# The fp32 doubling of the power tables on GpSimd in place of VectorE, with a higher threshold for early exponentials

## The chip, the cores and the metric

The kernel runs on one core of a Trainium2 chip. The core has TensorE (PE, matrix products), VectorE (DVE), ScalarE (ACT), GpSimd (POOL) and SyncE (SP, which issues DMAs here). The metric is the time of one execution on the device in microseconds (us).

## The reference, cut to what matters

Two mixers over the same x (2048 positions, 512 channels) are blended by a gate. A is attention with 32 heads of 16. B is a long convolution whose kernel is a sum of 128 complex powers per channel.

```python
x = A_x
g = _sigmoid((x * gate_w).sum(-1, keepdims=True))
a = _A_ref(x, A_wqkv, A_wo)      # scores -> softmax -> o @ wo, S = 2048, D = 512, H = 32
b = _B_ref(x, ...)               # dt = exp(log_dt); P = exp(dt*A*l); K = Re sum_n C*P*dB;
                                 # y = causal convolution of u with K, + u*Dskip
return g * a + (1 - g) * b
```

Inputs and output are bf16.

## The kernel before, in words

**Attention.** There are 32 blocks (4 quarters of 512 queries, 4 groups of 8 heads, 2 halves of a group), each of 16 key tiles by 4 row groups of PE: 2048 score tiles of 128 keys by 512 queries. Tiles go in groups of three, NG = 683 groups. For group g, `qk` writes three score banks (SC), `ex` (L913) is one exponential on ScalarE from SC to a ring of 15 tiles (ET), and `pv` multiplies ET by the values (VE) into one PSUM bank, OA. When a block ends, `norm_a` (L984) transposes OA on VectorE into OT, which frees OA for the next block; `norm_b` and `norm_c` normalise.

**Early sets.** For some key tiles VectorE computes the four exponentials itself, in a two-instruction approximation on bit patterns: `bits` (L949) turns a score bank into DZ, and `batch` (L960) makes two more shifted copies, DU and DZ, per set of four tiles. So a set is six VectorE instructions, and four groups have two tiles on ScalarE in place of three. `decide` starts a set only in the windows of groups in WIN (from group 180 on), only for the key tiles in VKT (four of sixteen per block up to group 640, then seven), and only if the idle time that the planner counts for VectorE has grown by a threshold. That threshold is `dvq()`: the first entry of DVQ whose flag is set (`scan1`, `scan0`, `S15`), else the last entry.

**The convolution.** `params` (all on VectorE) computes per channel the step L1 and the powers L2, L4, L8, then VL, marks `L8`, and goes on to L16, L32, L48 and their bf16 copies D16, D32, D48 (L1151). `base(qr)` builds for quarter qr (128 channels) a table of 16 consecutive powers in fp32 by doubling: two copies into FP (L1181), then products with L2, L4 and L8 into ft1 and ft2 and their sums and differences (all of them through the helper at L1007), and last a cast into the bf16 table B16 (L1204). `bases` runs the four quarters one after another. `table` multiplies B16 by D16, D32 and D48 in bf16 for pairs of blocks (eight pairs, two for each quarter): two copies (L1228) and 18 products and sums into PT, which goes to DRAM (`ptd`). A pair after the first waits for the kernel matrices (`K`, `kstage`, L1278) of the pair before it. `qload` reads PT back transposed (Qt), `sstage` makes the chunk states (from group 195 for blocks 0 to 7, from group 260 for 8 to 15; evicted at L1310), `scan` runs a recurrence over 30 chunks, twice, on VectorE (L1333 to L1340) with a DMA per chunk from GpSimd's queue (L1342), and `ystage` makes the outputs.

**What sets the order.** A planner writes out each engine's instruction stream in advance. Every step is a generator that yields the engine and an assumed duration; `Sched.fill` picks, engine by engine, what can start first, ties by priority. A product on 128 x n fp32 elements is booked with `dv(n)`:

```python
def dv(n, r=1):
    return .07 + n / 960 / r
```

whatever the engine, and each result with 0.085 us of latency. `AFTER` conditions order the planning alone; on the chip an instruction waits for semaphores of the data and the buffers that it uses. Each engine runs its stream in order.

Of the kernel before, what the change touches and what calls it, by code (L numbers as in the profile page):

```python
# [49 lines left out]
VSP = [len(k) * VSW for k in VKT]  # L50
VSAT = (168, 600)
WIN = ((180, 400, 2, 1), (400, 640, 2, 1), (640, 678, 3, 2))
DVQ = (("scan1", 0.2), ("scan0", 0.8), ("S15", 2.0), (None, 0.7))
BP = 2.2
DVCAP = 2.0
BUP = 1
# [33 lines left out]
class Prog:  # L90
# [107 lines left out]
    def op(self, eng, fn, R=(), W=(), c=.1, lat=.085, a=0, cfg=None):  # L198
        if self.cap is not None:
            self.cap.append((self.op, (eng, fn, R, W), dict(c=c, lat=lat, a=a, cfg=cfg)))  # L200
            return
        if cfg is not None:
            if cfg != self.cfg:
                c += TURN[cfg]
            self.cfg = cfg
        self.act += a
        self.log.append((self.op, self.q, (eng, fn, R, W)))
        deps = self._deps(eng, R, W)
        i = self.cnt[eng]
        at = self.tm[eng]  # L210
        for s, k in deps.items():
            at = max(at, self.fin[(s, k)] + (.03 if s == eng else .05))
        self.tm[eng] = at + c
        if eng == "DVE":
            self.busy += c
        self.fin[(eng, i)] = at + c + lat
        self.cnt[eng] += 1
        self._record(eng, fn, deps, eng, i, R, W)
        return at + c + lat
# [392 lines left out]
def dv(n, r=1):  # L612
    return .07 + n / 960 / r


def record(nc, p, B, ins):
# [135 lines left out]
    def dvq():  # L752
        return next(n for f, n in DVQ if f is None or f in sch.flag)

# [251 lines left out]
    def tt(eng, o, a, b_, f, R, W, c):  # L1006
        op(eng, lambda v: v.tensor_tensor(o(), a(), b_(), f), R, W, c=c)  # L1007
# [4 lines left out]
    def key(*ns):  # L1012
        return [(B[n], 0) for n in ns]
# [158 lines left out]
        sch.mark("scanpar")  # L1172

    def base(qr, eng):
        yield ("AFTER", "L8")
        FP, t1, t2, B16 = B["FP"], B["ft1"], B["ft2"], B[f"B16{qr}"]
        d0 = 128 * qr
        e8 = 128 * 8
        for l, n in ((0, "VV"), (1, "VL")):
            yield (eng, .38)  # L1180
            op(eng, lambda v, l=l, n=n: v.tensor_copy(FP(l, [[e8, 2], [8, 128]]), B[n](d0, [[D, 2], [1, 128]])), key(n), [(FP, 0)], c=.34)  # L1181
        for m, ln in ((2, "L2"), (4, "L4"), (8, "L8")):
            L = B[ln]
            for ch0 in range(0, 128, 64 if m == 8 else 128):
                nch = 64 if m == 8 else 128
                x = lambda ch0=ch0, m=m, nch=nch: FP(8 * ch0, [[e8, 2], [8, nch], [1, m]])
                ts = m * nch
                for ti, ri in ((t1, 0), (t2, 1)):
                    yield (eng, dv(2 * ts))
                    tt(eng, lambda ti=ti, ts=ts, nch=nch, m=m: ti(0, [[ts, 2], [m, nch], [1, m]]), x,  # L1190
                       lambda ri=ri, ch0=ch0, nch=nch, m=m, L=L: L(ri * D + d0 + ch0, [[0, 2], [1, nch], [0, m]]), ALU.mult,
                       [(FP, 0), (L, 0)], [(ti, 0)], dv(2 * ts))
                for part, f in ((0, ALU.subtract), (1, ALU.add)):
                    if m < 8:
                        o = lambda part=part, m=m: FP(part * e8 + m, [[8, 128], [1, m]])
                        W = [(FP, 0)]
                    else:
                        o = lambda part=part, ch0=ch0: B16(part * 2048 + ch0 * 16 + 8, [[16, 64], [1, 8]])
                        W = [(B16, (1, ch0))]
                    yield (eng, dv(ts))  # L1200
                    tt(eng, o, lambda part=part, ts=ts, nch=nch, m=m: t1(part * ts, [[m, nch], [1, m]]),
                       lambda part=part, ts=ts, nch=nch, m=m: t2((1 - part) * ts, [[m, nch], [1, m]]), f, [(t1, 0), (t2, 0)], W, dv(ts))
        yield (eng, 1.2)
        op(eng, lambda v: v.tensor_copy(B16(0, [[2048, 2], [16, 128], [1, 8]]), FP(0, [[e8, 2], [8, 128], [1, 8]])),  # L1204
           [(FP, 0)], [(B16, 0)], c=1.2)
        sch.mark(f"base{qr}")
# [439 lines left out]

    def bases():
        for qr in range(4):
            yield from base(qr, "DVE")

    for th, pr in ((norms(), 0), (qms(), 0), (projs(), 1), (gate(), .8), (ystage(), 2), (yloads(), 4), (params(), 2), (vscaled(0), 2.2), (vscaled(1), 2.2), (scan(), 3),
                   (bases(), BP), (table(), 2), (ublocks(), 4), (xyloads(), 4), (early(), 1.5), (reload(), 5), (outs(), 6)):
        sch.add(th, pr)
# [126 lines left out]
```

## Time and profile before

| what | value |
|---|---|
| median of the timed runs | 854.03 us (853.03 to 855.03, 2 runs) |
| the profiled execution, span from first to last instruction (no other time is listed for it) | 854.3 us |
| ScalarE busy | 826.1 us, 97%, 695 instructions |
| VectorE busy | 766.1 us, 90%, 1271 instructions |
| TensorE busy | 756.7 us, 89% |
| GpSimd busy | 44.0 us, 5%, 73 instructions |
| mean granted TensorE clock | 0.985 |

Busy time is the union of an engine's instructions. A row of a group of instructions gives the line, the engine, the operation, output<-inputs with shapes, the count, the busy time in us and the mean ns of one, and then the idle time just before them with what ended it. A row of the timeline gives the start and length in us. Lines of helpers (L1007, L632) carry many steps: tell them apart by the tiles.

### The profile page before, as it was taken

The page shows a single profiled execution, that of the slowest core. Times are in us where ns is not written, and L with a number is a line of the kernel's source. Part 1 is how long each engine was busy: PE and PEld are TensorE (multiplying, and loading weights), DVE is VectorE, ACT ScalarE, POOL GpSimd, SP SyncE. Part 2 cuts the span into 40 slices and gives each one's busy share as a digit, 9 for nine tenths or more (in the row PEclk, how much of TensorE's full clock was granted, in tenths as well). Part 3 has the DMA queues.
Part 4 walks back from the last instruction along what each step waited for, and adds up shares of the span by engine and source line. Part 5 has one row for each costly group of instructions (what it writes and reads, how often), then busy time and mean ns, then how long its engine had stood idle before and what let it go on. Part 6 is the DMA issues. An engine that isn't in the chain of part 4 may idle for free.

```text
span 854.3 us, 23568 instructions
## 1 busy us (share of the span) xinstructions
PE 756.7 (89%) x10301; PEld 296.5 (35%) x10301; DVE 766.1 (90%) x1271; ACT 826.1 (97%) x695; POOL 44.0 (5%) x73
## 2 busy tenths in 40 slices
PE   7888888788768999999999899889988899999986
PEld 3232332222212434343443344334442234443321
DVE  5799999999969988898898999999999978997994
ACT  6999999999979999999999999999999999999996
POOL 4000000000000000000010111101111100000000
PEclk9999999999989999899998999999999999999999
DMA  9400102942933498477394597248998425645120
GB/s 206 118 2 10 35 3 82 194 153 81 73 129 152 51 206 103 149 131 164 62 162 71 84 192 116 36 104 166 199 191 151 120 88 121 136 120 113 25 99 26
DMA packets 218168, 94.55 MB, mean 111 GB/s; under 512 B 185168, under 2 KB 205008, under 8 KB 216016
## 3 DMA queue, kind: packets, MB, share of 16 engines
q1 hardware_dynamic: 207408, 83.99, 45.6%
q0 software_dynamic: 8640, 7.87, 5.9%
q8 instruction: 81, 1.33, 0.6%
q10 hardware_dynamic: 2016, 1.18, 0.6%
q14 instruction: 23, 0.19, 0.1%
HBM read 35.17 MB, written 30.82 MB: 77 GB/s over the span
## 4 chain that ended last, share of the span: by engine, by line
ACT 66%; PE 23%; DMA 5%; DVE 4%; SPq 1%; issue 0%; ACTq 0%; DVEq 0%
ACT ET L913 65%; PE OA L632 9%; PE SC L632 7%; PE MB L632 7%; DMA gm_gd<-g 3%; DMA gm_ytd<-Yst 1%; DMA gm_ptd<-PT 1%; DVE DZ L949 1%; DMA Wq<-in_A_wqkv_dram 1%; DVE s L1333 1%; DVE s L1335 1%; DVE G L1340 0%; DVE s L1338 0%; DVE tt L1007 0%; SPq L1488 0%
## 5 line engine op out<-in xcount | busy, mean ns | idle before, releaser
L913 ACT ACTIVATE ET<-SC 128x1536 bf16<-128x1536 f32 (+1 forms) x683 | 817.8, 1508 | 15.1 <-PE SC L632 13.9
L632 PE MATMUL SC<-Qm,KT 32*128 32x512 bf16 x2048 | 276.5, 387 | 75.9 <-ACT ET L913 61.1
L632 PE MATMUL OA<-wm 128*32 128x256 bf16 (+3 forms) x2193 | 251.6, 341 | 1.2 <-DVE wm L685 1.2
L632 PE MATMUL OA<-ET,VE 128*32 128x512 bf16 x1800 | 181.6, 395 | 4.6 <-DVE OT L984 4.4
L949 DVE TENSOR_SCALAR DZ<-SC 128x512 uint16<-128x512 f32 x248 | 166.2, 685 | 19.1 <-PE SC L632 16.8
L632 PEld LDWEIGHTS SC<-Qm,KT 32*128 32x128 bf16 x2048 | 70.7, 91 | 291.8 <-ACT ET L913 233.9
L632 PEld LDWEIGHTS OA<-wm 128*32 128x32 bf16 (+2 forms) x2193 | 72.9, 95 | 33.8 <-issue 15.5
L632 PEld LDWEIGHTS OA<-ET,VE 128*32 128x32 bf16 x1800 | 46.1, 93 | 106.1 <-issue 98.4
L632 PE MATMUL MB<-X,Qt 64*128 64x32 bf16 x1024 | 74.5, 231 | 0.0
L632 PEld LDWEIGHTS MB<-X,Qt 64*128 64x128 bf16 x1024 | 57.7, 109 | 25.2 <-issue 23.0
L1310 DVE TENSOR_SCALAR SG<-MB 128x512 bf16<-128x512 f32 x64 | 43.9, 686 | 10.6 <-PE MB L632 9.8
L960 DVE TENSOR_SCALAR DZ<-DZ 128x2048 uint16<-128x2048 uint16 x62 | 42.5, 685 | 8.2 <-PE OA L632 8.2
L1342 POOL DMA_DIRECT2D SG<-G x60 | 33.0, 550 | 255.7 <-DVE G L1340 250.9
L1340 DVE TENSOR_TENSOR G<-s,s 128x512 f32<-128x512 f32 x60 | 41.2, 687 | 3.1
L960 DVE TENSOR_SCALAR DU<-DZ 128x2048 uint16<-128x2048 uint16 x62 | 42.3, 685 | 0.4
L1333 DVE TENSOR_TENSOR s<-G,MU 128x512 f32<-128x512 f32 x60 | 41.2, 687 | 1.0
L1338 DVE TENSOR_TENSOR s<-s,SG 128x512 f32<-128x512 f32 x60 | 41.1, 685 | 0.0
L1335 DVE TENSOR_TENSOR s<-G,MU 128x512 f32<-128x512 f32 x60 | 41.0, 683 | 0.0
L1007 DVE TENSOR_TENSOR ft<-FP,L 128x1024 f32<-128x1024 f32 (+1 forms) x32 | 34.4, 1084 | 0.1
L1007 DVE TENSOR_TENSOR PT<-tt,tt 128x1024 bf16<-128x1024 bf16 x48 | 32.8, 683 | 0.4
L632 PEld LDWEIGHTS MB<-Py,SG 128*32 128x32 bf16 x1024 | 29.6, 165 | 8.2 <-issue 4.1
L984 DVE STREAM_TRANSPOSE OT<-OA 128x512 f32<-128x512 f32 x32 | 22.8, 712 | 9.2 <-PE OA L632 8.8
(166 smaller groups left out, 625.6 us busy)
## 6 DMA issues: line engine op xcount, KB each, us to landing
gm_ptd<-PT SPq DMA_DIRECT2D x16, 1024.0 KB, 6.1
Py<-gm_ptd SPq DMA_DIRECT2D x32, 512.0 KB, 5.0
SG<-G POOLq DMA_DIRECT2D x60, 128.0 KB, 3.1
gm_kpd<-Kst SPq DMA_DIRECT2D x16, 256.0 KB, 3.5
Tt<-gm_kpd SPq DMA_DIRECT2D x128, 32.0 KB, 3.5
gm_xrd<-in_A_x_dram SPq DMA_DIRECT2D x1, 2048.0 KB, 13.2
X<-gm_xrd SPq DMA_DIRECT2D x8, 256.0 KB, 5.0
Wo<-in_A_wo_dram SPq DMA_DIRECT2D x4, 512.0 KB, 4.4
```

The lines of the kernel that those rows point to most:

```text
L632: op("PE", lambda t: t.matmul(out(), lhsT(), rhs(), start=start, stop=stop, skip_group_check=True, **kw), R, W, c=c, lat=.15, a=a, cfg=cfg)
L913: op("ACT", lambda a: a.activation(ET(512 * e, [[1, 512 * n]]), sc(0, [[1, 512 * n]]), AF.Exp, scale=DH ** -0.5), [(sc, i, g) for i in ran ...
L949: op("DVE", lambda v: v.tensor_scalar(z.u16(512 * k, [[1, 512 * n]]), sc(512 * na, [[1, 512 * n]]), XS, XB, ALU.mult, ALU.add), [(sc, na + ...
L960: op("DVE", lambda v: v.tensor_scalar(t.u16(0, [[1, 2048]]), z.u16(0, [[1, 2048]]), float(STEP[k][0]), None, ALU.add), R, W, c=.07 + 2048 ...
L984: op("DVE", lambda v: v.transpose(OT(512 * w, [[1, 512]]), OA(0, [[1, 512]])), [(OA, 0, b)], [(OT, w, b)], c=.64)
L1007: op(eng, lambda v: v.tensor_tensor(o(), a(), b_(), f), R, W, c=c)
L1310: op("DVE", lambda v, bank=bank, par=par, part=part: v.tensor_scalar(sg(2 * SGH + SGH * part + CB * k8 + 16 * par, [[2 * SGH, 32], [1, 16] ...
L1333: op("DVE", lambda v, g0=g0: v.tensor_tensor(s2(0, W), g0(0, W), MU(d0, [[0, 2], [1, 256]]), ALU.mult), [(g0, 0)] + key("MU"), [(s2, 0)], ...
L1335: op("DVE", lambda v, g0=g0: v.tensor_tensor(s3(0, W), g0(256, [[-256, 2], [1, 256]]), MU(D + d0, [[D, 2], [1, 256]]), ALU.mult), [(g0, 0) ...
L1338: op("DVE", lambda v, so=so: v.tensor_tensor(s2(0, W), s2(0, W), sg(so, W), ALU.add), [(s2, 0)] + ks, [(s2, 0)], c=F5)
L1340: op("DVE", lambda v, g1=g1: v.tensor_tensor(g1(0, [[1, 512]]), s2(0, [[1, 512]]), s3(0, [[1, 512]]), ALU.add), [(s2, 0), (s3, 0)], [(g1, ...
L1342: later("POOL", .3, 0, lambda so=so, g1=g1, c=c: dma("POOL", lambda e: e.dma_start(sg(so, [[1, 512]]), g1(0, [[1, 512]])), [(g1, 0)], [(sg ...
```

## The change

The doubling of all four quarters is issued to GpSimd. In the planning, quarters 2 and 3 may begin only when the tables of blocks 2 and 6 have been issued to their DMA. The last entry of DVQ, the threshold that holds until the flag `S15` or `scan0` is set, is 1.2 us in place of 0.7. The assumed durations are not changed.

```diff
-DVQ = (("scan1", 0.2), ("scan0", 0.8), ("S15", 2.0), (None, 0.7))
+DVQ = (("scan1", 0.2), ("scan0", 0.8), ("S15", 2.0), (None, 1.2))
...
     def base(qr, eng):
-        yield ("AFTER", "L8")
+        yield ("AFTER", f"pt{4 * qr - 6}" if qr >= 2 else "L8")
...
     def bases():
         for qr in range(4):
-            yield from base(qr, "DVE")
+            yield from base(qr, "POOL")
```

## The prediction

> **What bounds the kernel now.** I read the page's busy times first, then the exponentials by form, then all engines over six stages, then the same stages for L960 alone (two instructions for each early set on VectorE).
>
> ```profile
> PE 756.7 (89%) x10301; PEld 296.5 (35%) x10301; DVE 766.1 (90%) x1271; ACT 826.1 (97%) x695; POOL 44.0 (5%) x73
> ...
> L913 ACT ACTIVATE ET<-SC 128x1536 bf16<-128x1536 f32 x434 | 593.6, 1713 | 9.7 <-PE SC L632 9.3
> L913 ACT ACTIVATE ET<-SC 128x1024 bf16<-128x1024 f32 x249 | 242.0, 1151 | 5.4 <-PE SC L632 4.7
> ...
> 80.00:235.00 155.00, 126.29 (x1469) 41.26 (x1470) 151.14 (x245) 155.00 (x118) 0.00 (x0) 1.00 0.42 86
> 263.00:420.00 157.00, 150.83 (x1996) 64.28 (x1996) 140.74 (x236) 152.62 (x136) 1.05 (x2) 0.98 0.66 138
> ...
> 677.00:845.00 168.00, 153.72 (x2376) 58.98 (x2375) 141.56 (x233) 167.81 (x164) 0.53 (x1) 1.00 0.37 90
> ...
> 263.00:420.00 157.00, 23.68 (x35) 0.98 0.66 138
> 420.00:545.00 125.00, 8.88 (x13) 0.97 0.67 110
> 677.00:845.00 168.00, 40.45 (x60) 1.00 0.37 90
> ```
>
> The columns of the stage rows are PE, PEld, DVE, ACT and POOL with counts, then granted clock, DMA share and GB/s. ScalarE is busy 826.1 of the span's 854.3 us: the exponentials set the time. The span lies between the two timed runs (853.03 and 855.03), so I sum against 854.3 and add nothing around it.
>
> The time can fall in one way only, by more early sets: each takes four tiles off ScalarE. What one is worth: from 80 to 235 nearly all 118 activations have three tiles, 155.00 / 118 = 1.31 us each. From 677 to 845 there are 60 / 2 = 30 sets, so 120 activations of two tiles and 44 of three: (167.81 - 44 x 1.31) / 120 = 0.92 us. Four times 0.39 is 1.6 us a set. It can rise in one way too: VectorE being late with something that ScalarE needs.
>
> **The change, part by part.**
>
> *What VectorE loses.* All rows of the doubling, over four quarters, and some rows of its queue for the spacing:
>
> ```profile
> L1007 DVE TENSOR_TENSOR ft<-FP,L 128x1024 f32<-128x1024 f32 x24 | 29.0, 1217 | 0.1
> L1007 DVE TENSOR_TENSOR B<-ft,ft 128x512 bf16<-128x512 f32 x16 | 10.9, 683 | 0.1
> L1007 DVE TENSOR_TENSOR FP<-ft,ft 128x512 f32<-128x512 f32 x8 | 5.5, 686 | 0.1
> L1007 DVE TENSOR_TENSOR ft<-FP,L 128x512 f32<-128x512 f32 x8 | 5.5, 684 | 0.0
> L1204 DVE CAST B<-FP 128x2048 bf16<-128x2048 f32 x4 | 4.9, 1218 | 0.0
> L1007 DVE TENSOR_TENSOR FP<-ft,ft 128x256 f32<-128x256 f32 x8 | 3.3, 419 | 0.0
> L1181 DVE COPY FP<-VV 128x256 f32<-128x256 f32 x4 | 1.6, 397 | 0.0
> ...
> 79.92 0.39 DVE L1181 COPY FP<-VV 128x256 f32<-128x256 f32 x1
> ...
> 94.54 1.22 DVE L1007 TENSOR_TENSOR ft<-FP,L 128x1024 f32<-128x1024 f32 x1
> 95.67 0.68 DVE L1007 TENSOR_TENSOR L<-pt,pt 128x512 f32<-128x512 f32 x1
> 96.28 0.68 DVE L731 CAST VE<-MB 128x512 bf16<-128x512 f32 x1
> ...
> 99.62 0.42 DVE L1151 CAST D48.3_156<-L 128x512 bf16<-128x512 f32 x1
> ...
> 101.12 0.72 DVE L984 STREAM_TRANSPOSE OT<-OA 128x512 f32<-128x512 f32 x1
> ```
>
> With the four VL copies (as VV) these durations add to 62 us. Successive starts lie closer than durations (1.13 us behind a product of 1.22, 0.61 behind one of 0.68; for the shortest I take 0.3), so the queue gets back about 28 x 1.13 + 32 x 0.61 + 16 x 0.3 = 56 us.
>
> *What that is worth.* If all of it became sets, at six VectorE instructions of 0.685 us or 4.1 us each, it would be 13 sets and 21 us. It can't: no early set may start before group 180, which at 1.31 us each comes 236 us behind the first exponential, and the doubling is read by tables that begin at 122 us. What can move forward is the tables.
>
> ```profile
> L1007 DVE TENSOR_TENSOR PT<-tt,tt 128x1024 bf16<-128x1024 bf16 x48 | 32.8, 683 | 0.4
> ...
> L1228 DVE COPY PT<-B x16: 417/420/428, 122.4 to 360.5; 128x1024 bf16<-128x1024 bf16 x16
> L1310 DVE TENSOR_SCALAR SG<-MB x64: 652/691/693, 279.0 to 542.9; 128x512 bf16<-128x512 f32 x64
> L949 DVE TENSOR_SCALAR DZ<-SC x248: 649/684/694, 263.6 to 837.3; 128x512 uint16<-128x512 f32 x124
> ```
>
> The first early set is at 263.6 us. A pair of blocks costs VectorE 2 copies and 18 products, about 12 us, and eight pairs start 34 us apart ((360.5 - 122.4) / 7). A pair waits for the kernel matrices of the pair before it and for its PT tile to leave by DMA, so without the doubling between them I estimate 25 to 28 us: starts from 97 to about 285 in place of 122 to 360. Of the 56 us some 40 become idle VectorE time ahead of 235, where it buys nothing; one or two pairs, say 19 us, leave the stage 263:420. That stage has 157 - 140.7 = 16.3 us idle and 17.5 sets. With the same sharing at a threshold of 1.2, (16.3 + 19 + 17.5 x 4.1) / (4.1 + 1.2) = 20 sets. The threshold acts until S15 (last S eviction at 542.9), so in 420:545 I lose one of 6.5. Net two sets, 3 us gained. The S stages start no sooner, being gated at groups 195 and 260 and by PE at 150.8 of 157. The threshold alone would cost: 24 sets x 0.5 us of idle time, about two sets, 4 us the other way.
>
> *What GpSimd takes.* No GpSimd instruction in this trace reads a tensor. The nearest rows:
>
> ```profile
> L702 POOL MEMSET VE<- 128x2240 bf16 x4 | 7.7, 1964 | 0.3 <-DVE piota L690 0.3
> 0.24 0.10 POOL L1765 MEMSET const-float32-0.0<- 128x1 f32 x1 [0.24 <-issue]
> 273.67 0.52 POOL L1297 MEMSET SG<- 128x512 bf16 x1 [262.77 <-PE MB L632]
> ```
>
> One pass costs 1964 / 2240 = 0.88 ns per element, an empty instruction 0.1 us. A quarter is 16 products and sums with 10752 elements per partition, and 3 copies with 2560. One pass each: 12 + 1.9 = 14 us. Two passes for two-input forms: 19 + 2.2 + 1.9 = 23. Three passes (two for copies): 28.3 + 4.5 + 1.9 = 35. I take 29, between the last two, as each instruction also waits for the result of the one before, and keep 14 and 35. By the Trainium skill ("GPSIMD Engine Reference", section "Elementwise — side-by-side cycle accounting") 2048 fp32 elements of tensor_tensor take 4497 ns there against 2293 on VectorE; an estimate from that page is 27 us a quarter, and the sum below would be 2 us less. No run here shows it yet.
>
> *The new wait.* The planner books GpSimd at VectorE's costs: 14.2 us a quarter and about 0.1 us per link, so it expects quarter 0 at 79.9 + 16.4 = 96.3. VectorE's D48 copies end at about 100; without ten doubling instructions ahead of them (4.6 us) at 95.4. So pair 0's first copy is queued at about 97, but quarter 0 is there at 79.9 + 29 = 109: VectorE stands still 12 us. Behind it is the transpose of block 3's OA, at 101.1. What a late OA transpose costs, this trace shows once, in stage 235:263:
>
> ```profile
> 240.72 0.25 DVE L1279 TENSOR_SCALAR Kst<-MB,Dp 128x8 bf16<-128x8 f32 x1
> 244.74 0.43 DVE L1228 COPY PT<-B 128x1024 bf16<-128x1024 bf16 x1 [3.77 <-DMA gm_ptd<-PT]
> 247.18 0.43 DVE L1228 COPY PT<-B 128x1024 bf16<-128x1024 bf16 x1 [2.01 <-DMA gm_ptd<-PT]
> 250.78 0.71 DVE L984 STREAM_TRANSPOSE OT<-OA 128x512 f32<-128x512 f32 x1
> ...
> 251.54 0.62 PE L632 MATMUL OA<-ET,VE 128*32 128x512 bf16 x4 [4.38 <-DVE OT L984]
> ...
> 253.39 1.45 ACT L913 ACTIVATE ET<-SC 128x1536 bf16<-128x1536 f32 x1 [3.99 <-PE SC L632]
> 255.27 8.16 ACT L913 ACTIVATE ET<-SC 128x1536 bf16<-128x1536 f32 x6 [0.43 <-PE SC L632]
> ```
>
> VectorE waited 3.77 + 2.01 = 5.8 us, PE then 4.38 for OA, and ScalarE 3.99 + 0.43 = 4.4 for scores: PE runs in order, and the next scores are queued behind the product that needs OA. All but 1.4 us came through. So 12 us of standing cost 10.6. (At 14 us a quarter: nothing; at 35: 18 - 1.4 = 17.)
>
> *The later quarters* are covered: quarters 1 to 3 would be done at 138, 167 and 196, the pairs that read them start at about 97 + 2, 4 and 6 times 26.5 = 150, 203 and 256. The later begin of 2 and 3 is an order of planning; on the chip GpSimd goes on when its buffers are free. Nothing queues behind the doubling on GpSimd before the SG memset at 273.67. The 16 table writes and 16 kernel-matrix writes on SP go earlier and meet no queue that binds; the Qt loads wait for S stages as before.
>
> *The stall at 241 to 247* may vanish or come at another block end, as the pairs shift: 0, between -4 and +4.
>
> **Sum:** 854.3 - 3 + 10.6 = **862 us predicted**. Of this kernel a measurement can tell about 2%, 17 us, from no change: 837 to 871 is "same".
>
> **The rivals.**
>
> *Slower: the two engines block each other.* If a VectorE instruction that reads two SBUF tensors and a GpSimd one can't run together, the 76 GpSimd instructions (4 x 29 = 116 us) each hold up a table product. For it: from 80 on VectorE runs mostly such products. Against: VectorE would have those 40 us idle in that stretch, and its PSUM casts read one tensor:
>
> ```profile
> L722 DVE CAST Qs<-MB 128x512 bf16<-128x512 f32 x13 | 8.8, 679 | 1.0 <-PE MB L632 1.0
> L731 DVE CAST VE<-MB 128x512 bf16<-128x512 f32 x8 | 5.5, 688 | 0.6 <-PE MB L632 0.6
> ```
>
> 116 - 40 - 14 = 62 us is the most, by the same late transposes at each block end; with half of the meetings avoided, since GpSimd's instructions wait for each other and leave gaps, 31. It decides once the lateness at a block end passes 1.4 us. Time: 862 + 31 = 893, from 862 to 924. The trace of before neither shows nor excludes it: its GpSimd instructions read nothing. The Trainium skill ("SBUF — State Buffer", section "Who interferes with whom") says this will happen: an instruction of VectorE with two SBUF inputs contends with a GpSimd one that reads SBUF, and the loser waits for the whole instruction. By that rule this rival would be the forecast; I hold it lower because the blocking may fall into VectorE's idle time.
>
> *Faster, slightly: GpSimd keeps the booked time* (one pass, 14 us). No standing at 97: 854.3 - 3 and perhaps the 4 us at 241: 847. Against: it needs two reads and a write in the time of one write.
>
> *Faster by over 2%: the freed time does become sets.* 10 to 13 sets: 833 to 838. Against: the group gate at 180 and PE's 96% share from 263 to 420.
>
> *The change loses its purpose:* the threshold takes as many sets as the idle time gives; 862 + 3 = 865, no other verdict.
>
> **How the numbers follow.** Forecast with the last rival (851 to 868 by the ends of 14 and 35 us, 847 to 872 with the stall's 4): 0.55. Blocking: 0.30, of which 0.25 beyond 871. Booked time kept: 0.09. Sets: 0.06. A quarter of over 35 us adds 0.05 of the forecast's chance beyond 871. So faster 0.06, same 0.64, slower 0.30. The range 844 to 890 leaves out the sets (0.06) and the worse half of the blocking (0.14).
>
> **What would show it.** Right: in the trace of after a POOL span of doubling from about 80, a VectorE wait of 8 to 18 us for POOL on L1228 near 97, then a PE wait for OT and a ScalarE wait for SC of nearly that length; x64 to x66 on L960's DU form; tables ending near 300. Blocking: table products with starts further apart than 0.6 us while POOL is busy, and ScalarE waits at several block ends between 100 and 300. Wrong: no wait of VectorE for POOL, or over 68 sets. What would make it wrong at once is a quarter over 40 us on GpSimd, when quarters 1 and 2 come late as well, or an order in which the first copy lies behind the transpose.

## The result: 925.0 us, 8% slower, and the profile after

The changed kernel takes 925.02 us (median; 924.91 to 925.13) against 854.03 before: a ratio of 1.0825 (95% interval 1.0785 to 1.0865). The forecast of 862 was wrong, and so was the range of 844 to 890. The profiled execution has a span of 923.1 us.

The page of after, busy times and the costliest group:

```profile
PE 779.4 (84%) x10284; PEld 302.9 (33%) x10313; DVE 786.2 (85%) x1207; ACT 825.8 (89%) x695; POOL 169.6 (18%) x149
...
L913 ACT ACTIVATE ET<-SC 128x1536 bf16<-128x1536 f32 (+1 forms) x683 | 817.5, 1418 | 84.4 <-PE SC L632 79.1
```

ScalarE is busy as long as before (825.8 against 826.1 us), so all of the loss is idle time of ScalarE. Its largest kind of wait, in us in total, times and longest one, before and then after:

```profile
ACT ET L913 <- PE SC L632: 13.9, 26, 4.0
```

```profile
ACT ET L913 <- PE SC L632: 79.1, 53, 9.1
```

The wait for scores grew by 65 us; the time by 71. Where it sits is read from the stages, all engines (columns as in the prediction), before and then after:

```profile
80.00:150.00 70.00, 58.19 (x624) 20.67 (x624) 68.32 (x111) 70.00 (x54) 0.00 (x0) 1.00 0.14 40
150.00:235.00 85.00, 68.10 (x849) 20.60 (x850) 82.82 (x135) 85.00 (x65) 0.00 (x0) 1.00 0.65 123
```

```profile
80.00:150.00 70.00, 35.37 (x292) 12.12 (x295) 69.62 (x51) 34.72 (x26) 67.50 (x41) 0.68 0.01 3
150.00:235.00 85.00, 58.53 (x541) 17.37 (x543) 71.63 (x83) 62.37 (x47) 45.94 (x28) 0.82 0.41 114
263.00:420.00 157.00, 133.99 (x1694) 49.84 (x1694) 114.33 (x198) 143.16 (x118) 3.44 (x4) 0.95 0.50 111
```

From 80 to 150 VectorE is as full as before (69.62 of 70) and GpSimd nearly so (67.50), but VectorE gets 51 instructions done, not 111, and ScalarE works 34.72 us of 70: half of the whole loss in one stage. What VectorE does there, in the timeline (start, length):

```profile
86.85 2.25 DVE L1151 CAST D16.3_148<-L 128x512 bf16<-128x512 f32 x1
89.03 3.05 DVE L1007 TENSOR_TENSOR pt<-L 128x1024 f32<-128x1024 f32 x1
92.00 0.68 DVE L731 CAST VE<-MB 128x512 bf16<-128x512 f32 x1
...
115.08 1.38 DVE L1151 CAST D48.3_156<-L 128x512 bf16<-128x512 f32 x1
...
128.74 0.70 DVE L984 STREAM_TRANSPOSE OT<-OA 128x512 f32<-128x512 f32 x1
...
131.11 2.18 DVE L1228 COPY PT<-B 128x1024 bf16<-128x1024 bf16 x1
```

A cast of the kind that took 0.42 us before takes 2.25 and a 1024-element product 3.05 in place of 1.22, while the cast of VE, whose input is in PSUM, keeps its 0.68. D48.3 starts at 115.1, not 99.6, and block 3's transpose at 128.7, not 101.1. GpSimd in the same stretch, and its groups over the whole execution:

```profile
80.22 1.71 POOL L1181 COPY FP<-VL 128x256 f32<-128x256 f32 x1 [15.58 <-DVE VL L1007]
...
113.39 0.72 POOL L1181 COPY FP<-VV 128x256 f32<-128x256 f32 x1
```

```profile
L1007 POOL TENSOR_TENSOR ft<-FP,L 128x1024 f32<-128x1024 f32 x24 | 54.3, 2282 | 0.9
...
L1007 POOL TENSOR_TENSOR B<-ft,ft 128x512 bf16<-128x512 f32 x16 | 23.5, 1471 | 57.1 <-PE MB L632 28.6 <-DVE tt L1007 27.3
```

The first quarter takes 113.39 - 80.22 = 33 us, and the products run without gaps: 0.9 us idle before all 24 of them. Who is kept waiting by the late VectorE is told by the waits of PE:

```profile
PE MB L632 <- DVE VE L731: 19.4, 5, 6.9
PE MB L632 <- DVE KT L722: 19.4, 4, 9.8
PE OA L632 <- DVE OT L984: 12.1, 3, 5.9
PE MB L632 <- DVE Qs L722: 8.0, 3, 6.1
```

Together 59 us, against 4.4 (OT) and 0.8 (KT) before. The casts of projections are not stretched themselves; they are queued behind instructions that are. PE runs in order, so the next scores stand behind the projection that waits for its bank, and ScalarE behind the scores.

### The profile page after: what moved, and what is told of

Its sections match the earlier page's. It is cut to its first block, busy times and chain, and to the rows that moved or that the text cites. A ratio compares the mean times of both kernels' runs of the same rounds, so it can differ in the third digit from the quotient of the medians.

```text
span 923.1 us, 23602 instructions
## 1 busy us (share of the span) xinstructions
PE 779.4 (84%) x10284; PEld 302.9 (33%) x10313; DVE 786.2 (85%) x1207; ACT 825.8 (89%) x695; POOL 169.6 (18%) x149
## 4 chain that ended last, share of the span: by engine, by line
ACT 52%; PE 26%; DVE 17%; DMA 4%; issue 1%; SPq 1%; ACTq 0%; DVEq 0%
ACT ET L913 52%; PE OA L632 10%; PE SC L632 8%; PE MB L632 8%; DVE tt L1007 3%; DMA gm_gd<-g 2%; DVE PT L1007 1%; DVE DZ L949 1%; DVE pt L1007 1%; DVE u L1007 1%; DMA Wq<-in_A_wqkv_dram 1%; DMA gm_ptd<-PT 1%; DVE PT L1228 1%; DVE L L1007 1%; DVE KT L722 1%
## 5 line engine op out<-in xcount | busy, mean ns | idle before, releaser
L913 ACT ACTIVATE ET<-SC 128x1536 bf16<-128x1536 f32 (+1 forms) x683 | 817.5, 1418 | 84.4 <-PE SC L632 79.1
L632 PE MATMUL SC<-Qm,KT 32*128 32x512 bf16 x2048 | 285.5, 398 | 64.3 <-ACT ET L913 48.3
L632 PE MATMUL OA<-wm 128*32 128x512 bf16 (+3 forms) x2189 | 261.7, 357 | 1.2 <-DVE wm L685 1.2
L632 PE MATMUL OA<-ET,VE 128*32 128x512 bf16 x1792 | 185.0, 404 | 13.7 <-DVE OT L984 12.1
L949 DVE TENSOR_SCALAR DZ<-SC 128x512 uint16<-128x512 f32 x256 | 171.1, 684 | 26.1 <-PE SC L632 25.0
L632 PEld LDWEIGHTS SC<-Qm,KT 32*128 32x128 bf16 x2048 | 71.5, 91 | 287.8 <-ACT ET L913 206.6
L632 PEld LDWEIGHTS OA<-wm 128*32 128x32 bf16 (+2 forms) x2189 | 74.8, 97 | 38.1 <-issue 20.6
L632 PEld LDWEIGHTS OA<-ET,VE 128*32 128x32 bf16 x1792 | 46.3, 94 | 120.0 <-issue 100.8
L632 PE MATMUL MB<-X,Qt 64*128 64x32 bf16 x1024 | 74.1, 231 | 0.0
L1007 POOL TENSOR_TENSOR ft<-FP,L 128x1024 f32<-128x1024 f32 (+1 forms) x32 | 65.5, 2066 | 1.3
L632 PEld LDWEIGHTS MB<-X,Qt 64*128 64x128 bf16 x1024 | 57.8, 109 | 24.2 <-issue 21.8
L632 PE MATMUL MB<-Wv,xT 128*128 128x128 bf16 x256 | 23.1, 248 | 22.4 <-DVE VE L731 18.2
L1007 DVE TENSOR_TENSOR PT<-tt,tt 128x1024 bf16<-128x1024 bf16 x48 | 41.0, 854 | 1.0
L1007 POOL TENSOR_TENSOR B<-ft,ft 128x512 bf16<-128x512 f32 x16 | 23.5, 1471 | 57.1 <-PE MB L632 28.6
```

What stands on the lines that cost most here:

```text
L632: op("PE", lambda t: t.matmul(out(), lhsT(), rhs(), start=start, stop=stop, skip_group_check=True, **kw), R, W, c=c, lat=.15, a=a, cfg=cfg)
L913: op("ACT", lambda a: a.activation(ET(512 * e, [[1, 512 * n]]), sc(0, [[1, 512 * n]]), AF.Exp, scale=DH ** -0.5), [(sc, i, g) for i in ran ...
L949: op("DVE", lambda v: v.tensor_scalar(z.u16(512 * k, [[1, 512 * n]]), sc(512 * na, [[1, 512 * n]]), XS, XB, ALU.mult, ALU.add), [(sc, na + ...
```

## The experiments

Two theories. **Blocking:** a GpSimd instruction that reads SBUF and a VectorE product on two SBUF tensors exclude each other, VectorE falls behind where it has no idle time, and ScalarE waits. **Order:** the loss comes from late results of GpSimd (quarters of 33 us booked as 14), the later begin, the threshold, or where tiles are placed. Medians of before on the chips used were 855 to 856 us.

### The same idle GpSimd work, reading or only writing

Both keep the order of before and add scratch tiles DX and DY and, from `L8` on, 104 steps on GpSimd that nobody waits for:

```diff
+        for k in range(104):
+            yield ("POOL", 1.2)
# reading
+            op("POOL", lambda g: g.tensor_tensor(DY(0, [[1, 512]]), DX(0, [[1, 512]]), DX(512, [[1, 512]]), ALU.mult), ...)
# writing, twice in each step
+            op("POOL", lambda g: g.memset(DY(0, [[1, 512]]), 0.0), ...)
```

> The kernel before, its streams on all other engines in the same order, the doubling still on VectorE; from the point where L8 is there GpSimd runs 104 products of two SBUF tiles (bf16, 512 elements, an estimated 1.2 us each, some 125 us in all) into a tile that nobody reads, so nothing waits for it. Theory A (blocking: a VectorE instruction with two SBUF inputs or a fast SBUF copy and a GpSimd instruction that reads SBUF exclude each other): VectorE's products and copies between 80 and 250 us are stretched, PSUM casts are not, ScalarE waits at the block ends; 900 to 950 us. Theory B (late results: GpSimd takes 33 us a quarter where 14 are booked, and VectorE waits for them): nothing is late here, 854 within 0.5%. Theory C (the new order of the streams, with the threshold, is bad by itself): order unchanged, 854.

> As the run with idle products, but GpSimd only writes: 208 memsets of 512 bf16 elements (0.52 us each by the memset of the state tile, some 110 us in all) that nobody waits for. Theory A in the form that only reading GpSimd instructions block products: products keep 0.68 and 1.22 us, SBUF copies may be stretched a little; 854 to 862. If any GpSimd instruction blocked VectorE: as the run with products, over 890. Theories B and C: 854.

Measured: reading 943.63 us, 1.1017 (1.0961 to 1.1073); writing 870.46, 1.016 (1.0092 to 1.0228). Groups by form, of the reading kernel (VectorE's rows from 80 to 235 us):

```profile
L1656 POOL TENSOR_TENSOR DY<-DX 128x512 bf16<-128x512 bf16 x104 | 157.4, 1514 | 54.9 <-issue 46.8
...
L1007 DVE TENSOR_TENSOR ft<-FP,L 128x1024 f32<-128x1024 f32 x12 | 21.5, 1803 | 0.1
L1007 DVE TENSOR_TENSOR PT<-tt,tt 128x1024 bf16<-128x1024 bf16 x6 | 7.7, 1276 | 0.0
```

and of the writing kernel, whose memsets stand on two lines (L1657 has the other 104, 55.9 us), with a row of its timeline:

```profile
L1656 POOL MEMSET DY<- 128x512 bf16 x104 | 59.1, 568 | 5.9
...
L1007 DVE TENSOR_TENSOR ft<-FP,L 128x1024 f32<-128x1024 f32 x22 | 26.6, 1220 | 0.1
L1007 DVE TENSOR_TENSOR PT<-tt,tt 128x1024 bf16<-128x1024 bf16 x18 | 12.4, 686 | 0.0
L1151 DVE CAST D16.1_146<-L 128x512 bf16<-128x512 f32 x1 | 0.8, 821 | 0.0
```

```profile
236.50 0.69 DVE L1007 TENSOR_TENSOR B<-ft,ft 128x512 bf16<-128x512 f32 x1 [15.16 <-DMA gm_gd<-g]
```

The work that reads stretches both products by 0.59 us on the mean and costs 943.6 - 870.5 = 73 us, with order and tiles alike and nobody waiting for its result. The work that writes leaves them at 1220 and 686 (its memsets end at 138 us; the next experiment has some up to 235). At 870 it lies above the 854 to 862 expected: what it costs is nearly all one wait of 15.16 us for a transfer, which the reading kernel has too (14.9); the section on the threshold alone explains it.

The stretch is not an even slowing. VectorE's queues in the two kernels are the same instruction by instruction, and of the 76 two-input products and sums on SBUF tiles from 80 to 235 us, 45 are longer by 0.9 to 1.0 us and 12 not at all. The same sum, reading and then writing:

```profile
124.32 1.64 DVE L1007 TENSOR_TENSOR L<-pt,pt 128x512 f32<-128x512 f32 x1
```

```profile
100.43 0.68 DVE L1007 TENSOR_TENSOR L<-pt,pt 128x512 f32<-128x512 f32 x1
```

Over the whole queue the stretch adds to 74 us, and the spans of these two executions differ by 74 us as well.

### The change with the doubling reduced to writes

In the kernel after, each copy, product and cast on GpSimd becomes two memsets of half the booked time (writes), or one of a single element, the 512-element B tiles and the cast excepted (short):

> The changed kernel, every engine but GpSimd in the same order; on GpSimd each instruction of the doubling is replaced by two memsets of its output (same waits, about the same time: 0.9 us per 1024 elements twice), so the powers themselves are left out. Theory A: without reads VectorE's products are not stretched; results are still late, so 855 to 875. Theory B: as late as in the changed kernel, 910 to 930. Theory C: 910 to 930.

> The changed kernel in the same order, with the doubling on GpSimd reduced to memsets of one element, and of the B16 tile in one pass (about 5 us a quarter): the powers are left out, the waits stay, and GpSimd's results come earlier than booked. It shows what the freed VectorE time and the threshold are worth without any price. Theories A and B: 845 to 853 (64 sets for 62). Theory C: near 925.

Measured: writes 871.94, 1.0178 (1.0125 to 1.0231); short 864.38, 1.009 (1.0063 to 1.0118). Products of the writes kernel, and a cast of the short one:

```profile
L1007 DVE TENSOR_TENSOR PT<-tt,tt 128x1024 bf16<-128x1024 bf16 x26 | 17.8, 686 | 0.6
```

```profile
L1151 DVE CAST D16.2_147<-L 128x512 bf16<-128x512 f32 x1 | 2.1, 2105 | 0.0
```

With after's order and GpSimd busy for 108.6 us from 80 to 235, but only writing, 53 of the 71 us are gone; with the results early as well, another 7.6. The writes kernel's quarters take less time than after's (quarter 0 is ready at 110.8 us, not 113.4), so the 7.6 us bound the price of late results only roughly; VectorE waits for GpSimd there for 1.7 us in all. The one cast of 2.1 us in the short kernel falls beside a GpSimd memset of a B tile, which takes 1.9 us on the mean.

The short kernel missed the 845 to 853 expected. ScalarE waits 21.8 us for scores in it, against 13.9 in before; why isn't known, so 8 to 10 of after's 71 us have no cause shown.

These two kernels hold after's order itself: VectorE's 1207 instructions and ScalarE's 695 are the same, one by one. Paired so, VectorE's instructions up to 331 us take 60 us longer in after than in short, and after takes 60.6 us longer. All along its queue VectorE is late by about the stretch so far. One cast shows it, in after and in short (whose lines from L1227 on are one lower):

```profile
234.77 0.69 DVE L1278 CAST Kst<-MB 128x512 bf16<-128x512 f32 x1 [1.17 <-PE MB L632]
```

```profile
175.80 0.69 DVE L1277 CAST Kst<-MB 128x512 bf16<-128x512 f32 x1 [1.90 <-PE MB L632]
```

It comes 59.0 us later in after, behind 58.8 us of stretch, and ScalarE's exponential at that point is 59.4 us late.

### Honest bookings

```diff
+        dvp = lambda n: .1 + n * 2.15e-3     # in place of dv(n) for GpSimd; copies .72, casts 2.1
```

> The changed kernel with GpSimd's instructions booked at about what they took (0.1 us + 2.15 ns per element, 0.2 us more for sums, 0.72 and 2.1 us for copies and the cast: 30 us a quarter in place of 14), so that the planner puts the tables behind them. Theory A (blocking): the 127 us of GpSimd's instructions still stretch VectorE's products, which the planner doesn't know: 885 to 930. Theory B (late results): the waits are planned now, 850 to 865.

Measured 903.75, 1.0559 (1.0525 to 1.0593): 21 us better than after, 49 worse than before. The stretch stays:

```profile
80.00:150.00 70.00, 48.35 (x395) 14.87 (x394) 67.79 (x61) 46.01 (x35) 54.92 (x33) 0.71 0.06 11
```

GpSimd now stands twice for VectorE in this stage (6.8 and 5.2 us), works 54.92 us in place of 67.50, and ScalarE gets 46.01 in place of 34.72. How much of the 21 us is a better order and how much fewer meetings isn't separated.

### Half of the quarters

```diff
-            yield from base(qr, "POOL")
+            yield from base(qr, "DVE" if qr >= 2 else "POOL")    # first two; the other way about, and threshold 1.0: last two
```

> The changed kernel with quarters 2 and 3 doubled on VectorE again (begun as late as in the change) and only 0 and 1 on GpSimd, 66 us of it from 80 to about 146. Theory A: half of the price, that is half of the 59 us between the changed kernel and the one with short GpSimd instructions, on top of 856 to 864: 885 to 900, with stretched products up to 146 us and none behind. Theory B: nearly the whole price, since quarter 0 is the one that VectorE waits for: 910 to 925.

> The other half: quarters 0 and 1 on VectorE, 2 and 3 on GpSimd, begun later; threshold 1.0 (1.2 doesn't fit into SBUF). Theory A: again half of the price, 880 to 900, with stretched products only while GpSimd is busy. Theory B: little, as quarters 2 and 3 are needed late: 855 to 865.

Measured: first two 894.88, 1.0452 (1.0427 to 1.0477); last two 878.2, 1.0263 (1.0237 to 1.0289). The stage in which GpSimd works, of the first two and of the last two:

```profile
80.00:150.00 70.00, 35.30 (x300) 12.13 (x296) 69.33 (x52) 35.19 (x26) 63.93 (x37) 0.73 0.01 4
```

```profile
150.00:235.00 85.00, 64.28 (x669) 17.52 (x669) 77.01 (x77) 68.36 (x51) 63.98 (x38) 0.80 0.43 108
```

64 us of GpSimd work took 34.8 us from ScalarE in the first stage and 16.6 in the second. In the other stage of each kernel ScalarE is at 84.05 of 85 and 70.00 of 70. Against the mean durations of before, VectorE's instructions in these stages are 39 us longer in the first kernel and 33 in the second (an estimate, form by form); the kernels lose 40 and 23 us. So the stretch is nearly the same; in the first kernel all of it came through, in the second not all. VectorE has 0.7 us left idle in the stage of the first and 8 in that of the second. At 878.2 the second lies just under the 880 to 900 expected.

### The threshold alone

The kernel before with the last threshold 1.0, since with 1.2 alone its tiles don't fit into SBUF.

> The kernel before with the last threshold at 1.0 in place of 0.7 and nothing else (1.2 doesn't fit into SBUF). If the threshold takes sets as I worked out (0.5 us more was two sets fewer, 4 us), 0.3 us more is one or two sets fewer, 2 us: 855 to 860. If it were a main part of the change's price: over 865.

Measured 864.43, 1.0095 (1.0072 to 1.0119): a miss, for one set fewer should cost 1.6 us. VectorE and then ScalarE:

```profile
235.28 0.69 DVE L1007 TENSOR_TENSOR B<-ft,ft 128x512 bf16<-128x512 f32 x1 [17.59 <-DMA gm_gd<-g]
```

```profile
254.99 1.45 ACT L913 ACTIVATE ET<-SC 128x1536 bf16<-128x1536 f32 x1 [16.01 <-PE SC L632]
```

The fourth quarter's B tile got the address at which g1 had been, and the transfer that reads it (to `gm_gd`, 21 us to landing) was still under way. So I kept that address free, first for this kernel:

```diff
     sbs = [b for b in bufs.values() if b.kind == "sb" and b.first is not None]
+    bufs["g1"].last += 40
```

> The kernel before with the last threshold 1.0, and g1's address kept free for 40 more steps, so that the fourth quarter's B tile is no longer placed where g1 was. If the 864.4 of the threshold alone came from that address: the 17.6 us VectorE wait for the transfer of the gate is gone, ScalarE's 16 us wait at 255 falls to 4 or less, and the time is 850 to 857 (one set fewer costs 1.6). If it came from the order that the threshold gives: 862 to 866 again.

Measured 855.38, 0.9984 (0.9958 to 1.0009). In this kernel lines from L632 on are one higher:

```profile
254.03 1.45 ACT L914 ACTIVATE ET<-SC 128x1536 bf16<-128x1536 f32 x1 [4.27 <-PE SC L633]
```

The stall is back at the size that before has (3.99), and the 9 us are gone: they were placement, not the threshold. The kernels with idle work have the same stall.

### After with one part undone

Later begin and threshold 1.2 as in after, the doubling on VectorE, g1's address kept free:

```diff
-            yield from base(qr, "POOL")
+            yield from base(qr, "DVE")
```

> The kernel after with one part undone: later begin of quarters 2 and 3 and the threshold 1.2 kept, the doubling on VectorE again (g1's address kept free, or it would not fit). Blocking theory: no GpSimd work, so no stretched products (ft 1217, PT sums 683), ScalarE waits in all of 12 to 25 us, time 850 to 868; the whole loss of the change lies in its GpSimd part. If the later begin or the threshold carries a part of the loss: over 875.

Measured 858.05, 1.0033 (1.0008 to 1.0058). ScalarE's wait and VectorE's sets:

```profile
ACT ET L914 <- PE SC L633: 11.5, 21, 3.5
```

```profile
L950 DVE TENSOR_SCALAR DZ<-SC x240: 645/684/714, 267.6 to 844.5; 128x512 uint16<-128x512 f32 x120
```

From it to after the program differs in the engine of the doubling and in g1's address alone: the time rises by 67.0 us and ScalarE's wait for scores by 79.1 - 11.5 = 67.6. But the planner writes another order for it (1259 VectorE instructions, not 1207), so 67 holds a change of order too; the pair of after and short, with 60.6, doesn't. Later begin and threshold, with the order that they bring, cost 2.5.

### Copies in place of products

As the reading kernel, but 208 copies of 512 elements, one input each:

> The kernel before, its order kept, with 208 idle GpSimd copies of 512 bf16 elements from one scratch tile to another: one tensor read, not two; the same two scratch tiles as in the two runs with idle work, so the same 15 us wait for the transfer of the gate is in it. If any GpSimd instruction that reads SBUF blocks VectorE's products: products stretched (ft of 1024 above 1500 ns, PT sums above 900 ns in 80:235), and about the 0.46 us per busy GpSimd us of the two-input run, so 870 + 60 to 90 = 930 to 960. If two inputs on both sides are needed: products at 1217 and 683 ns and 868 to 875.

Measured 913.65, 1.0685 (1.0624 to 1.0746).

```profile
L1656 POOL COPY DY<-DX 128x512 bf16<-128x512 bf16 x104 | 101.3, 974 | 6.4
...
L1007 DVE TENSOR_TENSOR ft<-FP,L 128x1024 f32<-128x1024 f32 x17 | 25.4, 1505 | 0.1
L1007 DVE TENSOR_TENSOR PT<-tt,tt 128x1024 bf16<-128x1024 bf16 x12 | 11.5, 958 | 0.0
```

One input on GpSimd is enough to block, as expected; the time, 914, is below the expected 930 to 960. Beside copies of 0.97 us a product is longer by 0.28 on the mean (by 0.4 where it is held up at all), and 202 us of them cost 43 over the writing kernel (VectorE's stretch adds to 44), 0.21 for each busy us; the two-input products cost 73 / 157 = 0.46. I had carried over the price per busy us, and it depends on the instruction.

### A lower threshold

Before with 0.6 in place of 0.7 and g1's address kept free, in search of a faster version:

> The kernel before with the last threshold 0.6 in place of 0.7 and g1's address kept free: looks for a version below both. If sets are taken out of idle VectorE time, up to one more set, 852 to 856; if a lower threshold makes VectorE late at block ends, 857 to 862.

Measured 853.88, 0.9977 (0.9953 to 1.0002): not told apart from before. No version here beats before by what can be measured.

## Why the prediction was wrong, step by step

**The step that failed is a term put at nothing.** The sum, 854.3 - 3 + 10.6, has no term for "the two engines block each other"; that stood as a rival with 0.30, at 893. It is what happens, and it is worth some 60 us. The Trainium skill's rule, named there ("SBUF — State Buffer", section "Who interferes with whom"), said so, and every trace here agrees: product against reading GpSimd stretched (686 to 1276 ns), against writing GpSimd not (686), a cast from PSUM untouched (0.68 us). I set it aside because "the blocking may fall into VectorE's idle time". The short kernel, in which VectorE has neither the doubling nor much blocking, shows that idle time by stage:

```profile
80.00:150.00 70.00, 57.54 (x625) 21.07 (x625) 63.25 (x101) 68.66 (x53) 15.18 (x56) 0.98 0.34 84
150.00:235.00 85.00, 66.53 (x800) 19.85 (x798) 52.67 (x92) 82.25 (x63) 5.85 (x20) 1.00 0.41 110
```

The 40 us exist (6.75 + 32.3 = 39), but 32 of them lie behind 150, and GpSimd does its first two quarters from 80 to 146. An average over 80:235 hid that. And of the 32, 20.1 are one wait for PE in short:

```profile
216.98 0.18 DVE L1469 COPY gp<-MB 128x16 f32<-128x16 f32 x1 [20.10 <-PE MB L632]
```

In after the same copy starts at 275.8 us, behind a wait of 18.7 us of which all but 8 lie behind the end of GpSimd's doubling (265.4). Most of the rest are short waits for PE before casts, and in after they come as late as all else. So in after the idle time took up nothing: 60 us of stretch made 60.6 us.

**The price inside the rival.** Its most, 116 - 40 - 14 = 62, made 924, and 925 came; that is luck. GpSimd worked 127 us, not 116, VectorE was held up for 60 of them, not for all, and neither the 40 us of idle time nor 14 us at block ends came off. The halving to 31 had the wrong reason: GpSimd's instructions leave no gaps (0.9 us idle before 24 products). About half of its time was met all the same (60 of 127), as it was by the idle products (74 of 157).

**The new wait** (12 us of standing at the first L1228 copy, 10.6 at ScalarE) didn't occur:

```profile
L1228 DVE COPY PT<-B x16: 417/420/2180, 131.1 to 374.6; 128x1024 bf16<-128x1024 bf16 x16
  DMA gm_ptd<-PT: 6.8, 2
```

VectorE never stood for GpSimd there; only the DMA is named. Quarter 0 was ready at 113.4, 4 us later than I had it (109), but the first copy came at 131.1, not 97. Two things put it there. VectorE had fallen 26.3 us behind; and in after's queue the copy lies behind block 3's transpose (128.7), an order that the prediction itself named as one that would make it wrong at once. In the short kernel, in the same order, the first copy is at 104.8:

```profile
L1227 DVE COPY PT<-B x16: 414/420/2043, 104.8 to 315.5; 128x1024 bf16<-128x1024 bf16 x16
```

The reckoning of the 97 also took ten doubling instructions out of VectorE's queue before D48; the trace of before has eight there, with the 4.6 us that I gave them.

**The path to ScalarE** was half right. I let it run through late OA transposes; they are 12.1 of PE's 59 us, and VE, KT and Qs casts 46.8. Any VectorE instruction that PE waits for is hit, not the one at the block end alone.

**What GpSimd takes:** 29 us a quarter was near: 33 measured under contention, and 24 x 2282 ns for the largest group, between the two and three passes I bounded with. The other estimate there, 27, lay further off.

**The later quarters** were not covered by buffers alone: GpSimd waited 27.3 us for a VectorE table product and 28.6 for PE before B tiles, and quarters 1 to 3 were done at 146, 205 and 265, not 138, 167 and 196. The pairs came late enough that this cost nothing seen: the first lay at 131, the last copy at 374.6, not near 300.

**What it is worth in sets** was right in count:

```profile
L949 DVE TENSOR_SCALAR DZ<-SC x256: 648/684/693, 326.3 to 909.0; 128x512 uint16<-128x512 f32 x128
```

256 / 4 = 64 sets against 62; with the doubling on VectorE the threshold and the later begin left 60, the two sets fewer that I gave the threshold. The 3 us forecast for them don't show: the price of a set stays unproven, as 61 and 62 sets (855.38 and 855.55) aren't told apart, and the short kernel, with 64, is not faster. **The stall at 241 to 247**, held at 4 us either way, was only half seen: one tile's address made it 16.

## What to carry to other kernels

Before work is moved to an idle GpSimd, list by stage which VectorE instructions run beside it. Where these are products on two SBUF tensors, and ScalarE hangs on VectorE by way of PE as here, ScalarE loses at most about as long as VectorE's instructions are stretched (60.6 us for 60, 73 for 74, 23 for 33). Idle time of VectorE in an average over stages is no cover: ask what it waits for, and whether GpSimd still works when that wait comes. A cheap trial is idle GpSimd work of the same kind, which nobody waits for, once reading and once writing only. And when an edit of a constant moves the time, look first whether a tile has got the address of one that a slow transfer still reads.

## What the runs showed of the hardware that was not expected

- GpSimd work that only writes leaves two-input products alone (686 ns) but can double VectorE's fast casts between SBUF tiles: seven of the twelve D casts take 0.81 or 0.82 us in the writing kernel where all take 0.42 in before, and in the short kernel one takes 2.1 beside a memset of 1.9.
- While ScalarE and PE were starved from 80 to 150, the granted clock of TensorE was 0.68, against 1.00 before, with PE busy half of the time. It left no loss of its own that can be seen: against the short kernel (0.98 there) after loses what VectorE's stretch adds to.
- In the writing kernel and the threshold's, a transfer of 8 KB to `gm_gd` takes 21 us to landing, as it does in before, where nothing waits for it.
